# The first spans of an attention and gated feed-forward kernel: instructions put out in the order of a table

## The chip, the cores and the metric

One Trainium2 core runs the whole program. The metric is device time in microseconds (us) of one execution. The trace is one profiled execution on the chip; the times are those of three other executions.

## The reference

```python
# q, k, v: 8 batches x 8 heads x 576 positions x 64, float32
q_s = softmax(q, axis=-1)             # over the 64 columns of a head
k_s = softmax(k, axis=2)              # over the 576 positions
kv = einsum('bhsd,bhse->bhde', k_s, v)
x = einsum('bhsd,bhde->bhse', q_s, kv).transpose(0, 2, 1, 3).reshape(4608, 512)
gate = 1 / (1 + exp(-(x @ w_gate)))   # 512 x 1536
val = x @ w_val                       # 512 x 1536
out = (gate * val) @ w_out            # 1536 x 512
```

The denominators of both softmaxes have 1e-9 added.

## The kernel before

The 4608 tokens are taken in nine spans of 512. A span w needs its 512 rows of x, the two products with w_gate and w_val (called `g1`), the sigmoid and the multiplication, and the product with w_out (`g2`). The 1536 inner columns are taken as 12 tiles j of 128, or six pairs p of tiles.

Span 0 goes tile by tile: `g1_0(j)` on TensorE, `g_sig_0` (L813, ScalarE) and `g_mul_0` (L817, VectorE) make h, and `g2_0(j)` (L855) adds its product with w_out. From tile 5 on the operands are split into a high and a low part, the high part copied on ScalarE, the low part subtracted on VectorE (`h_hi_0`, `h_lo_0`, `wo_hi` L255, `wo_lo` L259, `split_hi` L380, `split_lo` L385). Spans 1 to 8 go pair by pair by a scheme with seven products of sums of blocks (`g1`, L889, then L922 to L951 to put the results together, `g2`, L988). The sums of weight blocks (`w_sums`, L315) and their splits are made once, beside span 0, stored in DRAM, and read back by `s_load` (L399, L401), the first time for two of the pairs unsplit into x_32, and split on arrival (`sums_split`, L342 and L343).

Beside span 0 there is other work. The weights arrive as 64-bit words and are narrowed in four steps that go back and forth between two engines: `w_top` (ScalarE L173), `w_low` (VectorE L178), `w_sign` (ScalarE L187), `w_join` (VectorE L197), and the same as `wo_top`, `wo_low`, `wo_sign`, `wo_join` for w_out. And the attention of span 1 is made: the maxima of k (L428), gathered through a row in DRAM (`k_max_send` L450, `k_max_read` L456), `k_sub` (L482), `k_exp` (L487), `k_sum` (L437), `k_mm`; the maxima, exponentials and sums of q (`qn_max` L594, `qn_sub` L601, `qn_exp` L605, `qn_sum` L611 to L617). For span 2 the maxima of q go to DRAM with `qn_send` (L586) and come back with `q_spread` (L626).

Nothing plans the order: each engine executes its instructions in the order in which the program calls them, and waits at one whose operand is not ready, with all that stands behind it. SP issues the loads, the stores of the result (`acc_out`, L841), `qn_send` and `q_spread`; POOL issues the stores and loads of the split weights. Each of these two queues is in order too, and the transfer that one issues waits for the eighth before it on the same queue. ScalarE needs another function table between an exponential and a sigmoid (ACT_TABLE_LOAD). The calls of span 0 stand in a loop over j whose body calls the steps of different tiles and of the attention in a fixed sequence.

Of the kernel before, what the change touches and what calls it, by code (L numbers as in the profile page):

```python
# [47 lines left out]
C_PAIRS = {T1: T2, B21: T3, B22: T4}  # L48


@with_exitstack
def attn_moe(ctx: ExitStack, tc: tile.TileContext, q0_in, qf, qn, qT, k0T_in, v0_in, k, kT, v, w_in, wo, out):
    nc = tc.nc
# [51 lines left out]
    ctx.enter_context(tc.manual_schedule())  # L105

# [41 lines left out]

    def load_w(j):
        w_raw[j] = t = raw_tile(j)  # L150
        src = w_in[j].bitcast(I32)
        if j:
            nc.sync.dma_start(out=t, in_=src)
        else:
            for n in range(2):
                nc.sync.dma_start(out=half_of(t, n), in_=half_of(src, n))

    def load_wo(j):
# [60 lines left out]

    def w_top(j, n=None):  # L220
        narrow_top(raw_of(j, n), w_of(j, n))

    def w_low(j, n=None):
        w_bits[j, n] = narrow_low(raw_of(j, n))

    def w_sign(j):
        narrow_sign(w_bits[j, None], w_of(j, None))

    def w_join(j, n=None):
        narrow_join(w_bits.pop((j, n)), w_of(j, n))  # L230
# [5 lines left out]

    def wo_top(j):
        if j % 2 == 0:
            wo_t[j // 2] = wtpool.tile([P, 2, DM], F32, name="wo_t")
        narrow_top(in_two(wo_raw[j]), wo_f32(j))  # L240

    def wo_low(j):
        wo_bits[j] = narrow_low(in_two(wo_raw.pop(j)))

    def wo_sign(j):
        narrow_sign(wo_bits[j], wo_f32(j))

    def wo_join(j):
        narrow_join(wo_bits.pop(j), wo_f32(j))

    wo_out = {}

    def wo_hi(j):
        wo_out[j] = t = whpool.tile([P, 2, DM], F32R, name="wo_hl")
        nc.scalar.copy(out=halves(t[:, 0]), in_=apart(wo_t[j // 2][:, j % 2]))  # L255

    def wo_lo(j):
        t = wo_out[j]
        nc.vector.tensor_tensor(  # L259
            out=halves(t[:, 1]), in0=apart(wo_t[j // 2][:, j % 2]),  # L260
            in1=halves(t[:, 0].bitcast(F32)), op=ALU.subtract,
        )

    def wo_store(j):
        t = wo_out[j]
        nc.gpsimd.dma_start(out=wo_dram[j], in_=t.rearrange("p h e -> p (h e)").bitcast(F32))
# [3 lines left out]

    def wo_keep(j):
        nc.gpsimd.dma_start(out=wo_dram[j][:, DM:], in_=wo_t[j // 2][:, j % 2])
# [4 lines left out]

    def wo_load(w, p):
# [13 lines left out]

    def wo_split(w, p):
# [14 lines left out]

    def w_sums(p):
# [20 lines left out]

    def sums_keep(p):
# [4 lines left out]
    s_stage = {}  # L336

    def sums_split(p, parts=range(4)):
# [5 lines left out]

    def sums_store(p, parts=range(4)):
        n = 4 * 2 * P
# [26 lines left out]

    def split_hi(p, parts=(*SUMS, FIRST, LAST)):
# [6 lines left out]

    def split_lo(p, parts=(*SUMS, FIRST, LAST)):
# [11 lines left out]

    def s_load(p, i, first):
# [19 lines left out]

    def kT_load(b, hp, t=None):
# [17 lines left out]

    def k_sum(b, hp):
# [6 lines left out]

    def k_max_turn(b):
        k_turned[b] = ps = ps_at.tile([P, T], F32, name="at")[:NP, 0:P]
        nc.tensor.transpose(ps, kneg[b], ident)

    def k_max_send(b):
# [5 lines left out]

    def k_max_read(b):
# [4 lines left out]

    def k_load(b, t, kt=None):  # L460
# [5 lines left out]

    def v_load(b, t, vt=None):
# [10 lines left out]

    def k_sub(b, t, eng=nc.vector):
# [3 lines left out]

    def k_exp(b, t):
# [5 lines left out]

    def k_tr_0(hp):
# [10 lines left out]

    def k_get_0(hp):
# [7 lines left out]

    def k_mm_0(ps):
# [10 lines left out]

    def k_mm(b, t):
# [12 lines left out]

    def k_done_0(ps):
# [6 lines left out]

    def k_done(b):
# [8 lines left out]

    def kv_split(b, kv):
# [20 lines left out]

    def qn_load(w, c):
# [3 lines left out]

    def qn_send(w, what):
# [6 lines left out]

    def qn_max(w, c):
# [5 lines left out]

    def qn_sub(w, c, eng=nc.vector):
# [23 lines left out]

    def q_spread(w, what, hp):
# [19 lines left out]

    def qf_tr(w, hp, ps):
# [32 lines left out]

    def x_mm(w, hp):
# [14 lines left out]

    def x_ev(w, hp):
# [6 lines left out]

    def qT_copy(hp):
# [38 lines left out]

    def c_subs():
# [11 lines left out]

    def c_split_hi(i):
# [9 lines left out]

    def c_split_lo(i):
# [20 lines left out]

    def g1_0(j):
# [33 lines left out]

    def h_lo_0(j):
# [5 lines left out]

    def acc_out(w):  # L830
# [12 lines left out]

    def g2_0(j):
# [33 lines left out]

    def g1(w, p, s_next=None):
# [74 lines left out]

    def h_split(w, p):
# [12 lines left out]

    def g2(w, at):
# [219 lines left out]

    kT_sb_0 = [k0T[:, hp] for hp in range(NP)]  # L1190
# [43 lines left out]

    def q_sub_0(i):
# [305 lines left out]
```

## Time and profile before

| | |
|---|---|
| median of three executions | 905.75 us (904.39 to 906.54) |
| the profiled execution | 904.38 us |
| its span | 902.5 us |
| TensorE busy | 880.3 us, 98% |
| VectorE, ScalarE, GpSimd busy | 616.6 us, 500.9 us, 184.0 us |
| granted TensorE clock | 1.0 in all windows |

The span is the part of an execution in which the profiler sees instructions; 1.88 us of the profiled execution lie around it. TensorE is busy nearly always, so the rows below list the places where it is not. A row of a timeline has the start of a run of equal instructions, its length, the engine, line, tiles and count, and in brackets the idle time ahead of it and what ended that. Engines are PE (TensorE), DVE (VectorE), ACT (ScalarE), POOL (GpSimd) and SP.

### The profile page before, as it was taken

The numbers are of one execution on the slowest core, as the hardware profiler recorded it, in microseconds if no ns is written. First come the engines' busy times: TensorE is split into PE (matmuls) and PEld (weight loads), VectorE is DVE, ScalarE is ACT, GpSimd is POOL, SyncE is SP. The second block draws the span as 40 slices with busy tenths as digits, with TensorE's granted clock in tenths as the row PEclk, the third lists the DMA queues.
The fourth block names the chain that finished last, engine by engine and source line by source line (L and its number), as shares of the span: only waits on it lengthen the run. The fifth ranks groups of instructions, "written<-read, shape, count | busy, mean of one in ns | idle before, by whom it ended". The sixth has DMA issues, their size and how long they took to land.

```text
span 902.5 us, 16614 instructions
## 1 busy us (share of the span) xinstructions
PE 880.3 (98%) x6533; PEld 799.0 (89%) x6533; DVE 616.6 (68%) x966; ACT 500.9 (56%) x842; POOL 184.0 (20%) x342
## 2 busy tenths in 40 slices
PE   8998888999999999999999999999999999999998
PEld 6444776999999999999999999999999999999997
DVE  8879879878967577666767677666856674664242
ACT  5895677567656456644664466455735443553222
POOL 0102102333221312212221222112122122212220
PEclk9999999999999999999999999999999999999999
DMA  9997545998999979996999799978997799868772
GB/s 334 391 349 249 192 187 189 330 309 264 328 359 286 328 244 352 350 297 213 336 325 325 221 333 341 334 227 284 345 303 240 230 273 325 245 191 261 223 213 70
DMA packets 88966, 252.62 MB, mean 280 GB/s; under 512 B 12892, under 2 KB 13176, under 8 KB 87480
## 3 DMA queue, kind: packets, MB, share of 16 engines
q0 software_dynamic: 45200, 163.08, 57.1%
q1 hardware_dynamic: 43688, 88.47, 31.6%
q8 instruction: 52, 0.85, 0.4%
q14 instruction: 26, 0.21, 0.1%
HBM read 217.97 MB, written 33.54 MB: 279 GB/s over the span
## 4 chain that ended last, share of the span: by engine, by line
PE 71%; DVE 11%; DMA 7%; ACT 6%; issue 4%; POOL 1%; SPq 0%; DVEq 0%; POOLq 0%; ACTq 0%
PE gv L889 43%; PE acc L988 25%; DMA s<-s_sb 3%; DMA s_sb<-s 2%; PE gv L688 1%; PE at L532 1%; DMA x<-s 1%; DVE s L315 1%; DVE k_neg L428 1%; DMA kmax_b<-kmax_row 1%; DVE a_w L385 1%; DMA lent<-q_in 1%; ACT ring L487 1%; ACT w_raw L187 1%; DVE f_w L197 1%
## 5 line engine op out<-in xcount | busy, mean ns | idle before, releaser
L889 PE MATMUL gv<-c_hl,s_sb 128*128 128x256 f32 x2304 | 275.4, 276 | 2.0 <-DMA s_sb<-s 1.0
L889 PEld LDWEIGHTS gv<-c_hl,s_sb 128*128 128x128 f32 x2304 | 265.9, 192 | 3.4 <-issue 1.6
L889 PE MATMUL gv<-c_hl,a_w 128*128 128x256 f32 x1728 | 217.2, 275 | 1.6 <-DVE c_hl L768 1.3
L889 PEld LDWEIGHTS gv<-c_hl,a_w 128*128 128x128 f32 x1728 | 204.8, 192 | 2.7 <-DVE c_hl L768 1.6
L401 POOL DMA_DIRECT2D s_sb<-s x164 | 89.4, 545 | 274.2 <-PE gv L889 256.6
L988 PE MATMUL acc<-wo_hl,h 128*128 128x512 f32 x589 | 135.5, 380 | 0.0
L988 PEld LDWEIGHTS acc<-wo_t,h 128*128 128x128 f32 x613 | 115.5, 189 | 16.3
L988 PE MATMUL acc<-wo_t,h 128*128 128x512 f32 (+1 forms) x613 | 129.7, 362 | 0.0
L935 DVE TENSOR_TENSOR sg<-gv,sg 128x512 f32<-128x512 f32 x48 | 33.1, 690 | 132.5 <-PE gv L889 132.5
L988 PEld LDWEIGHTS acc<-wo_hl,h 128*128 128x128 f32 x589 | 107.7, 189 | 13.6
L937 ACT COPY sg<-gv 128x512 f32<-128x512 f32 x48 | 28.1, 586 | 95.6 <-PE gv L889 95.6
L922 ACT COPY sg<-gv 128x512 f32<-128x512 f32 x48 | 28.2, 587 | 91.3 <-PE gv L889 91.3
L940 DVE TENSOR_TENSOR sg<-sg 128x512 f32<-128x512 f32 x48 | 33.2, 692 | 52.0 <-ACT sg L937 52.0
L961 DVE TENSOR_TENSOR h<-sg,h 128x1024 fp32r<-128x1024 f32 x48 | 58.9, 1226 | 1.7
L949 DVE TENSOR_TENSOR sg<-sg 128x512 f32<-128x512 f32 x48 | 33.2, 692 | 36.6 <-ACT sg L943 36.6
L943 ACT ACTIVATE sg<-sg 128x512 f32<-128x512 f32 x48 | 30.2, 630 | 44.8 <-DVE sg L942 44.8
L289 POOL DMA_DIRECT2D wo_hl<-wo x44 | 23.8, 541 | 151.6 <-PE acc L988 151.6
L931 ACT COPY sg<-gv 128x512 f32<-128x512 f32 x48 | 28.2, 587 | 35.6 <-PE gv L889 35.6
L928 ACT COPY sg<-gv 128x512 f32<-128x512 f32 x48 | 28.1, 585 | 29.4 <-PE gv L889 29.4
L289 POOL DMA_DIRECT2D wo_t<-wo x45 | 24.8, 550 | 93.1 <-PE acc L988 91.9
L805 PE MATMUL gv<-x,f_w 128*128 128x512 f32 x96 | 42.0, 592 | 0.0
L805 PEld LDWEIGHTS gv<-x,f_w 128*128 128x128 f32 x96 | 18.2, 190 | 23.0 <-issue 21.5
(182 smaller groups left out, 1188.2 us busy)
## 6 DMA issues: line engine op xcount, KB each, us to landing
s_sb<-s POOLq DMA_DIRECT2D x164, 512.0 KB, 6.7
wo_t<-wo POOLq DMA_DIRECT2D x45, 512.0 KB, 6.7
wo_hl<-wo POOLq DMA_DIRECT2D x44, 512.0 KB, 5.5
s<-s_sb POOLq DMA_DIRECT2D x24, 512.0 KB, 7.6
out<-x SPq DMA_DIRECT2D x35, 256.0 KB, 6.8
ring<-k_in SPq DMA_DIRECT2D x28, 256.0 KB, 8.5
ring<-qn_in SPq DMA_DIRECT2D x28, 256.0 KB, 5.5
q_b<-q_m_row SPq DMA_DIRECT2D x56, 128.0 KB, 8.7
```

Of the source, the lines that this page charges most:

```text
L289: nc.gpsimd.dma_start(out=t.rearrange("p h e -> p (h e)"), in_=wo_dram[j].bitcast(F32R))
L401: nc.gpsimd.dma_start(out=s_of(i).rearrange("p h n e -> p (h n e)"), in_=s_dram[p][:, i * n:(i + 1) * n].bitcast(F32R),)
L805: nc.tensor.matmul(ps[n], lhsT=a, rhs=x, start=(kt == 0 and i == 0), stop=(kt == NK - 1 and i == len(pairs) - 1),)
L889: nc.tensor.matmul(ps[:, n], lhsT=lh(kt), rhs=woven(c_hl[i][:, x, kt]), start=(first and n == 0 and kt == 0 and lh is wh and x == 0), stop ...
L922: nc.scalar.copy(out=sg[:, 0], in_=y)
L931: nc.scalar.copy(out=sg[:, 1], in_=y)
L935: nc.vector.tensor_tensor(out=sg[:, 0], in0=rr, in1=sg[:, 0], op=ALU.add)
L940: nc.vector.tensor_tensor(out=sg[:, 3], in0=sg[:, 3], in1=sg[:, 2], op=ALU.add)
L943: nc.scalar.activation(sg[:, 0:2, 0], sg[:, 0:2, 0], AF.Sigmoid)
L949: tt(out=sg[:, 0:2, 0], in0=sg[:, 0:2, 0], in1=sg[:, 0:2, 1], op=ALU.mult)
L961: nc.vector.tensor_tensor(out=lo, in0=sg[:, :, 0], in1=hi.bitcast(F32), op=ALU.subtract)
L988: nc.tensor.matmul(acc[w][m][:, es], lhsT=h[lh][:, i, sl], rhs=woven(o[i][:, rh])[:, ts], start=(at == 0 and i == 0 and lh == 0 and rh == ...
```

## The change

A class records the calls of the program from the first load on, up to pair 2 of span 1, as instructions with the name of the step that calls them, its numbers and a count (`wo_low.5`, `k_exp.1.0`, `g1_0.3@4` for the first four matmuls of a step). At pair 2 it puts them out in the order of one table. What is computed does not change, and TensorE's own order does not either. The order on VectorE changes up to about its 240th instruction, on ScalarE up to the 209th, on the SP queue up to the 85th, on POOL up to the 67th. ScalarE has 46 table loads in all where it had 44: among its first 92 instructions there are eight where there were four, and later two fewer.

```diff
+class Steps:
+    def keep(self, engine, call):
+        name = self.names[-1]
+        last = self.kept[-1] if self.kept else None
+        if engine == "tensor" and last and last[:2] == (engine, name):
+            last[3].append(call)
+            return
+        n = self.count[name] = self.count.get(name, -1) + 1
+        self.kept.append((engine, name, f"{name}:{n}" if n else name, [call]))
+
+    def put(self, order):
+        kept, self.kept = {t: calls for _, _, t, calls in self.kept}, None
+        for t in order.split() or list(kept):
+            name, _, n = t.partition("@")
+            calls = kept[name]
+            for _ in range(int(n or len(calls))):
+                calls.pop(0)()
...
+ORDER = """
+top top:1 top:2 top:3 top:4 top:5 v_load.0.4 load_w.0 load_w.0:1 load_wo.0 top:10 load_w.1 load_wo.1 top:11
...
+"""
...
     ctx.enter_context(tc.manual_schedule())
+    nc = Steps(nc)
...
+    @named
     def load_w(j):
...
     nc.gpsimd.memset(ones, 1.0)
+    nc.kept = []
...
         for at in range(NS):
+            if (w, at) == (1, 2):
+                nc.put(ORDER)
             p = step(w, at)
```

Every instruction that went through the table has line 89 after the change. The first place is ScalarE around the sigmoid of tile 3 (h_0_565 before, h_0_235 after; ring are the rows of k, kt its transposed form, lent another part of that, wo_t and wo_raw w_out, w_raw and f_w the gate and value weights). Before:

```order
L487 ACTIVATE ring_374<-ring_374 128x512
L487 ACTIVATE ring_376<-ring_376 128x512
L487 ACTIVATE ring_378<-ring_378 128x512
L487 ACTIVATE ring_380<-ring_380 128x512
L487 ACTIVATE ring_382<-ring_382 64x512
L437 ACTIVATE kt_0_117,k_sum_528<-kt_0_117,k_neg_527 128x576
L437 ACTIVATE kt_1_118,k_sum_528<-kt_1_118,k_neg_527 128x576
L813 ACT_TABLE_LOAD
L813 ACTIVATE h_0_565<-gv_535 128x512
L173 ACTIVATE wo_t_567<-wo_raw_458 128x512
```

After:

```order
L89 ACTIVATE ring_167<-ring_167 128x512
L89 ACT_TABLE_LOAD
L89 ACTIVATE h_0_228<-gv_224 128x512
L89 CAST w_raw_191<-f_w_227 128x2x512
L89 CAST kv_sb_114<-f_last_120 64x4x64
L89 ACTIVATE h_0_235<-gv_232 128x512
L89 ACTIVATE wo_t_236<-wo_raw_229 128x512
L89 ACTIVATE wo_t_236<-wo_raw_218 128x512
L89 CAST w_raw_203<-f_w_227 128x2x512
L89 ACT_TABLE_LOAD
L89 ACTIVATE lent_158,k_sum_205<-lent_158,k_neg_204 128x576 x2
L89 CAST wo_raw_202<-wo_t_217 128x2x256
```

The sigmoid of tile 3 moved ahead of the exponentials of k and of two of the row sums of k, directly behind that of tile 2, and a table load more stands between it and those.

The second place is VectorE around the multiplication of tile 3 (h_0_565 before, h_0_235 after), with the sums of q (q_r) and the split of x (x_hl). Before:

```order
L197 SCALAR_TENSOR_TENSOR wo_t_453<-wo_t_453,wo_raw_404 128x512
L178 TENSOR_SCALAR w_raw_406<-w_raw_406 128x2x512
L178 TENSOR_SCALAR wo_raw_458<-wo_raw_458 128x2x256
L726 TENSOR_TENSOR x_hl_153<-x_0_149,x_hl_152 128x1024
L561 TENSOR_TENSOR kv_sb_114<-f_last_120,kv_sb_114 64x4x64 x2
L611 TENSOR_REDUCE q_r_587<-ring_182 128x8
L611 TENSOR_REDUCE q_r_587<-ring_184 128x8
L611 TENSOR_REDUCE q_r_587<-ring_186 128x8
L611 TENSOR_REDUCE q_r_587<-ring_188 128x8
L616 TENSOR_SCALAR q_r_587<-q_r_587 128x32
L617 RECIPROCAL q_r_587<-q_r_587 128x32
L817 TENSOR_TENSOR h_0_565<-gv_536,h_0_565 128x512
```

After:

```order
L89 TENSOR_REDUCE k_neg_230<-kt_0_117 128x1
L89 SCALAR_TENSOR_TENSOR f_w_227<-f_w_227,w_raw_203 128x1024
L89 TENSOR_TENSOR s_32_213<-f_w_181,s_32_211 128x512
L89 TENSOR_TENSOR h_0_235<-gv_233,h_0_235 128x512
L89 SCALAR_TENSOR_TENSOR wo_t_236<-wo_t_236,wo_raw_229 128x512
L89 RECIPROCAL q_r_239<-q_r_239 128x32
L89 TENSOR_TENSOR ring_166<-ring_166,q_r_239 128x512
L89 TENSOR_SCALAR k_sum_205<-k_sum_205 128x4
L89 SCALAR_TENSOR_TENSOR wo_t_236<-wo_t_236,wo_raw_218 128x512
L89 TENSOR_TENSOR s_32_244<-s_32_243,f_w_200 128x512
L89 TENSOR_REDUCE k_neg_230<-kt_1_118 128x1
L89 SCALAR_TENSOR_TENSOR wo_t_217<-wo_t_217,wo_raw_202 128x512
```

The multiplication no longer stands behind four sums of q; wo_t_217, the w_out tile of tile 3, is joined eight rows behind it, and the other steps moved out from between.

The third place is the SP queue at the end of span 0, where the results of span 0 (out) are stored, the maxima of q go out (q_m_row) and come back (q_b). Before:

```order
L477 DMA f_last<-v_in 128x512 x2
L477 DMA f_last<-v_in 64x512
L477 DMA v_116<-v_in 128x512
L841 DMA out<-x_112 128x512 x4
L586 DMA q_m_row<-q_m 128x32
L626 DMA q_b<-q_m_row 64x512 x8
```

After:

```order
L89 DMA q_m_row<-q_m 128x32
L89 DMA out<-x_112 128x512
L89 DMA ring<-k_in 128x512
L89 DMA out<-x_112 128x512
L89 DMA v_116<-v_in 128x512
L89 DMA q_b<-q_m_row 64x512
L89 DMA out<-x_112 128x512 x2
L89 DMA kt_118<-kT_in 128x576
```

The store of the maxima moved ahead of the four stores of the result, and one reading of them back (q_b) now stands ahead of the last two of these stores.

## Rows read from the trace of the kernel before

**Rows 1.** Part 1 of the page: busy time, share, instructions.

```profile
PE 880.3 (98%) x6533; PEld 799.0 (89%) x6533; DVE 616.6 (68%) x966; ACT 500.9 (56%) x842; POOL 184.0 (20%) x342
```

**Rows 2.** Windows; PE, PEld, DVE, ACT, POOL busy (count), granted clock, DMA share, GB/s.

```profile
23.50:68.40 44.90, 44.88 (x106) 19.54 (x104) 35.26 (x52) 39.09 (x58) 5.94 (x10) 1.00 0.99 370
68.40:181.30 112.90, 99.73 (x574) 79.83 (x575) 98.35 (x154) 73.70 (x112) 23.25 (x41) 1.00 0.64 229
181.30:902.50 721.20, 716.01 (x5684) 683.84 (x5682) 463.89 (x734) 373.98 (x647) 153.97 (x285) 1.00 0.92 281
```

**Rows 3.** Timeline of TensorE: start, length, what, idle time ahead and releaser.

```profile
61.35 7.03 PE L805 MATMUL gv<-x,f_w 128*128 128x512 f32 x16
71.85 3.70 PE L855 MATMUL acc<-wo_t,h 128*128 128x512 f32 x8 [3.47 <-DVE h L817]
...
110.29 5.94 PE L805 MATMUL gv<-x_hl,a_w 128*128 128x512 f32 x24 [1.38 <-ACT v L813]
...
148.07 2.86 PE L855 MATMUL acc<-wo_hl,h_parts 128*128 128x512 f32 x12 [0.29 <-ACT h_parts L821]
...
152.38 1.49 PE L889 MATMUL gv<-c_hl,a_w 128*128 128x256 f32 x11 [1.35 <-DVE c_hl L768]
...
155.76 1.60 PE L889 MATMUL gv<-c_hl,s_sb 128*128 128x256 f32 x12 [0.55 <-ACT sg L922]
...
162.84 2.75 PE L855 MATMUL acc<-wo_hl,h_parts 128*128 128x512 f32 x12
...
171.85 3.11 PE L889 MATMUL gv<-c_hl,s_sb 128*128 128x256 f32 x24 [0.59 <-DMA s_sb<-s]
...
182.66 2.84 PE L889 MATMUL gv<-c_hl,s_sb 128*128 128x256 f32 x24
```

**Rows 4.** Waits of TensorE over the span: total, times, longest.

```profile
PE acc L855 <- DVE wo_hl L259: 3.1, 3, 1.1
PE gv L805 <- DVE a L385: 2.2, 2, 1.7
```

**Rows 5.** Chain of waits from 40 to 75 us: start, length, what.

```profile
50.66 6.69 DMA kmax_b<-kmax_row
...
58.10 3.03 ACT ring L487 x5
...
62.66 1.28 ACT L813
63.96 0.60 ACT h L813
...
68.18 2.48 DVE q_r L611 x4
...
71.16 0.63 DVE h L817
```

**Rows 6.** Lines by form, VectorE, 23.5 to 68.4 us: busy time, mean ns.

```profile
L197 DVE SCALAR_TENSOR_TENSOR f_w<-f_w,w_raw 128x1024 int32<-128x1024 int32 x2 | 2.4, 1220 | 1.1 <-ACT w_raw L187 1.1
...
L315 DVE TENSOR_TENSOR s<-f_w 128x512 f32<-128x512 f32 x2 | 1.4, 684 | 0.0
```

**Rows 7.** Timeline of VectorE from 160 to 170 us.

```profile
167.55 2.45 DVE L594 TENSOR_REDUCE q_m<-ring 128x8 f32<-128x512 f32 x4
```

**Rows 8.** Waits of the SP queue, 20 to 200 us: total, times, longest.

```profile
SPq L626 <- DMA q_m_row<-q_m: 8.1, 1, 8.1
```

**Rows 9.** Timeline of the SP queue from 160 to 185 us.

```profile
165.59 3.11 SPq L841 DMA_DIRECT2D out<-x  x4
```

**Rows 10.** DMA issues from 148 to 153 us: size, us to landing.

```profile
kmax_b<-kmax_row POOLq DMA_DIRECT2D x1, 256.0 KB, 4.0
kmax_row<-kmax_b POOLq DMA_DIRECT2D x1, 2.0 KB, 2.8
```

**Rows 11.** DMA issues from 150 to 190 us: size, us to landing.

```profile
x<-s POOLq DMA_DIRECT2D x8, 256.0 KB, 6.6
out<-x SPq DMA_DIRECT2D x4, 256.0 KB, 9.0
```

More of the change, by code (lines that the diff above doesn't have):

```diff
@@ L48, with __init__ @@
 C_PAIRS = {T1: T2, B21: T3, B22: T4}
+class Steps:
+    def __init__(self, nc):
+        self.kept, self.names, self.count = None, ["top"], {}
+        for e in ("tensor", "vector", "scalar", "gpsimd", "sync"):
+            setattr(self, e, Engine(self, e, getattr(nc, e)))
+    def keep(self, engine, call):
[13 more added lines that the diff above has]
+                calls.pop(0)()
+        assert not any(kept.values()), [t for t, calls in kept.items() if calls]
@@ new lines, with __init__, __getattr__, call @@
+class Engine:
+    def __init__(self, steps, name, engine):
+        self.steps, self.name, self.engine = steps, name, engine
+    def __getattr__(self, op):
+        do = getattr(self.engine, op)
+        def call(*args, **kw):
+            if self.steps.kept is None:
+                do(*args, **kw)
+            else:
+                self.steps.keep(self.name, lambda: do(*args, **kw))
+        return call
+ORDER = """
+top top:1 top:2 top:3 top:4 top:5 v_load.0.4 load_w.0 load_w.0:1 load_wo.0 top:10 load_w.1 load_wo.1 top:11
@@ new lines @@
+split_hi.4.1.2.3.4:2 wo_sign.10 g1_0.9@12 g_sig_0.9 top:23 w_sign.11 qT_split.1.3:1 g1_0.9 g_mul_0.9
+w_join.11 split_lo.5.0 split_hi.4.1.2.3.4:1 g2_0.8 split_hi.4.1.2.3.4:3 split_lo.4.1.2.3.4:2
+split_hi.4.1.2.3.4 x_mm.1.3 h_hi_0.9 split_lo.4.1.2.3.4 split_hi.5.6.5 split_lo.4.1.2.3.4:4 wo_hi.9
+wo_join.10 split_lo.4.1.2.3.4:5 wo_lo.9 split_lo.4.1.2.3.4:1 wo_hi.10 split_lo.4.1.2.3.4:3 h_lo_0.9 x_ev.1.3
+wo_store.9 wo_low.11 c_split_hi.0 w_sums.5 split_hi.5.6.5:1 c_split_lo.0 g1_0.10@12 g_sig_0.10 w_sums.5:2
@@ new lines @@
+g1_0.10 split_lo.5.6.5:1 split_lo.5.6.5 c_subs:2 split_hi.5.1 w_sums.5:1 wo_sign.11 g2_0.9 g_mul_0.10
+split_lo.4.1.2.3.4:6 h_hi_0.10 wo_lo.10 split_hi.5.2.3.4:1 split_hi.5.2.3.4 w_sums.5:3 wo_load.1.4:1 top:22
+split_lo.4.1.2.3.4:7 c_subs:1 h_lo_0.10 c_subs:3 g1_0.11 split_lo.5.2 k_max_turn.2 c_split_hi.1 split_lo.5.1
+split_lo.5.2:1 c_split_hi.4 wo_store.10 g_sig_0.11 split_lo.5.1:1 c_split_hi.2 g_mul_0.11 g2_0.10
+c_split_lo.1 c_split_lo.4 g1.1.5.4 g1.1.5.4:1 c_split_lo.2 c_split_hi.3 wo_join.11 g1.1.5.4:2
@@ L105, in attn_moe, with named, step @@
     ctx.enter_context(tc.manual_schedule())
+    nc = Steps(nc)
+    def named(f):
+        def step(*args, **kw):
+            numbers = [a for x in args for a in (x if isinstance(x, tuple) else (x,)) if isinstance(a, (int, str))]
+            nc.names.append(".".join(map(str, (f.__name__, *numbers))))
+            f(*args, **kw)
+            nc.names.pop()
+        return step
     def r(ap):
@@ L240, in wo_top @@
         narrow_top(in_two(wo_raw[j]), wo_f32(j))
+    @named
     def wo_low(j):
         wo_bits[j] = narrow_low(in_two(wo_raw.pop(j)))
+    @named
     def wo_sign(j):
         narrow_sign(wo_bits[j], wo_f32(j))
+    @named
     def wo_join(j):
```

127 lines of the change are left out of this document (added).

## Prediction

> **What bounds the kernel now.** I read part 1 of the page first: TensorE is busy for 880.3 of 902.5 us [rows 1], so whatever the order does, at most 22 us are to be had. The windows say where. From 181.3 us on, beyond the table's reach on TensorE, TensorE is busy for 716.0 of 721.2 us, and from 23.5 to 68.4 us for 44.88 of 44.90; in between it idles for 112.90 − 99.73 = 13.2 us [rows 2]. The granted clock is 1.00 in all three. The timeline of TensorE then shows this idle time as eleven waits: 3.47, 1.09, 1.38, 1.03, 0.57, 1.00, 1.67, 0.29, 1.35, 0.55 and 0.59, together 12.99 us [rows 3, 4]. I call them a to k; b, d and f are the three for wo_hl, and e and g the two for `a`, that rows 4 add up. Ten of them end on an instruction of VectorE or ScalarE, the last on a DMA. VectorE is busy for 35.26 of 44.90 and then for 98.35 of 112.90 us, ScalarE for 39.09 and 73.70 [rows 2]: neither is full, so the waits come from what stands ahead of the operand that is wanted, and an order can remove them.
>
> The longest, a, is followed on the chain of waits [rows 5]. The maxima of k land at 50.66 + 6.69 = 57.35. Five subtractions begin there, and ScalarE then does five exponentials (3.03), two row sums, the table load (1.28), and only then the sigmoid of tile 3, at 63.96. VectorE, having got its next piece from ScalarE, still does splits and four sums of q (2.48) ahead of the multiplication of tile 3, which starts at 71.16. TensorE had finished the matmuls before its need at 61.35 + 7.03 = 68.38 [rows 3].
>
> **The change part by part.** TensorE keeps its order and its matmuls; all that can change is how long it waits. I went through the new order with the durations of the trace of before, each instruction behind its predecessor and its operands, against the times at which TensorE would need them without any wait.
>
> *Wait a.* In the new order the sigmoid of tile 3 follows that of tile 2, and the multiplication follows a join and a sum; of the five exponentials none stands ahead of the sigmoid, and the sums of q are done earlier. The last feed of `g2_0(3)` is then not the multiplication but the join of its w_out tile, eight rows behind. Up to it VectorE has 60 instructions from 23.5 us on: 42 of 0.68 us, 8 wide ones of 1.21, one reduction of 2.5, nine small ones of together 3.3, 44.2 us end to end; the two frequent sizes are those of [rows 6]. They overlap: four sums take 2.48, or 0.62 each [rows 5], which takes off 60 × 0.06 = 3.6. So 40.6 us of work stand in the 44.9 us up to 68.4. VectorE did 35.26 there and waited for 9.64 [rows 2]; it may now wait for 4.3. ScalarE has 45 instructions up to the piece that this join needs, 39 us end to end and 35 with a like overlap of 0.09, in the same 44.9. I get the join 1.9 us ahead of time: a goes, −3.47. If VectorE waits as much as before, 9.64 − 4.3 = 5.3 comes back, more than a; that end stays in the range.
>
> *Waits b to j.* Here the wanted low part, product or sum is moved forward among independent work. In the walk the operands come ahead of need by 1.1 (h_lo of tile 5), 0.9 and 2.5 (the blocks `a`), 1.6 (c_hl, the one behind the wait of 1.35), about 3 (wo_hl) and 1.2 to 2 (the rest). They sum to 8.93. The margins are of the size of one or two VectorE instructions (0.68 to 1.22 [rows 6]), and one handover that comes a row late costs that much. I let a fifth come back: +1.8. Bounds: 0, and all 8.9.
>
> *Wait k and the SP queue.* TensorE's product with the sums of the next pair starts at 182.66 in before [rows 3]; its second sum is wanted half of the 2.84 later, so at 184.1 − 13.0 = 171.1 without waits. It comes through a line of transfers that the change makes longer: the store of the maxima of q, then a reading of them back, then two stores of the result behind this in the SP queue, and only then can x_32 be loaded anew. In before that reading waits 8.1 us for the store to land [rows 8], but with all four stores of the result ahead; nothing of it is behind. After, `g2_0(11)` ends at 162.84 + 2.75 − 12.4 = 153.2 [rows 3], two copies and two reductions of 2.45 / 4 = 0.61 each follow [rows 7], and the store goes at 155.7. From there: landing, three issues on SP at 3.11 / 4 = 0.78, together 2.3 [rows 9], landing of the result, landing of the load, 1.3 for the split, two instructions of the shorter size of [rows 6]. With short landings, 2.8 for the store and 4.0 for each 256 KB [rows 10], this is 155.7 + 2.8 + 2.3 + 4.0 + 4.0 + 1.3 = 170.1, 1.0 early. With crowded ones, 8.1 [rows 8], 9.0 and 6.6 [rows 11], it is 183.0, 11.9 late. The store now goes ahead of the four results, so its landing is nearer to 2.8; the other two are in the same traffic as before, and I take 6.6 for each: 175.3, 4.2 late, less the 1.8 by which TensorE is late by then, and less another 0.9, an estimate, because DMA is busy for only 0.64 of this window [rows 2] and 6.6 may be too long: +1.5. Wait k itself (0.59) goes.
>
> By the Trainium skill, "DMA: Bandwidth & Descriptors", section "Anatomy of one DMA — SWDGE (gpsimd) path", a DMA takes about 2.0 us and its bytes at 436 GB/s, 2.6 us for 256 KB. The 6.6 and 9.0 of [rows 11] don't agree, since other transfers run beside them. By the rule the line would end at 155.7 + 2.0 + 2.3 + 2.6 + 2.6 + 1.3 = 166.5, 4.6 us early, the term of 1.5 would be nothing, and the sum 1.5 lower.
>
> *Table loads.* Four more of them stand in ScalarE's first 92 instructions, two fewer later. One takes 1.28 us, and the sigmoid behind it starts 0.02 us after its end [rows 5], so 4 × 1.28 = 5.1 us of ScalarE, which the 5.8 us that it idles from 23.5 to 68.4 and the 39.2 us after that hide [rows 2]; those that fall ahead of the join are counted in its 35 us. Cost 0. The cover is gone where a sigmoid is late by more than its margin, 2.4 us at tile 2.
>
> The Trainium skill speaks against this: "ScalarE: Activation LUTs", "What ACT_TABLE_LOAD costs" and "Table sets: the hidden batching unit", counts 2.66 us for each switch, load and drain, and asks to batch by set. The row shows no drain of 1.38 us. By the page the four cost 10.6 us of ScalarE, and the margin of tile 2 shrinks by 1.4 for the one switch ahead of it; it is not used up.
>
> *Start and tail.* Up to 23.5 us the order is almost the same, and behind 181.3 us it is unchanged: 0.
>
> Sum: −12.99 + 1.8 + 1.5 = −9.7. The profiled execution took 904.38, so 894.7; the median of the shown runs lies 1.37 above it, so 905.75 − 9.7 = 896.0.
>
> **The rivals.** *A, half the waits return.* Margins of 1 to 2 us are small on two in-order engines that hand each piece back and forth. Half of 12.99 is 6.5: 899.3. For it: ten of the eleven waits are of this kind. Against: VectorE idles 24.2 us from 23.5 to 181.3 [rows 2], and 11 of them would remain without any wait on TensorE.
>
> *B, the SP queue replaces them.* If the landings are as in [rows 8, 11], TensorE waits up to 11.9 at the second sum; the 1.8 is inside this, so −12.99 + 11.9 = −1.1 and 904.7 at the far end, 898.7 with half of it. For it: these landings are from this very stretch. Against: the store no longer goes last.
>
> *C, slower: VectorE starves.* The place is 23.5 to 95 us, where each narrowing goes ScalarE, VectorE, ScalarE, VectorE, now with exponentials and table loads between, and where a load that lands late stops both engines in turn; some weights are now requested behind other loads, while DMA is at 0.99 of its time [rows 2]. It decides from the point where VectorE idles more than the 24.2 us of before up to the end of the table; each us above is one on TensorE. With 28 us it is 905.75 + 3.8 = 909.5. Against: VectorE would have to wait for 17 us more than the new order's work leaves.
>
> *D, given back later.* The main part needs DMA at 0.92 of its time [rows 2]; if it is this that sets its end, an earlier start only waits for loads: 905.75. Against: at 281 GB/s TensorE idles there for only 5.2 us in 721.
>
> **How the numbers follow.** Forecast 0.55, A 0.18, B 0.13, C 0.09, D 0.05. What a measurement of this kernel can tell from no change is about 0.2%, 1.8 us: faster means below 903.9. The forecast but for 0.01, A, and most of B (0.11) are faster, 0.83; D, 0.01 of the forecast and 0.02 of B are the same, 0.08; C is slower, 0.09. The lowest sum has neither term come back and half a us more of the start: 905.75 − 13.0 − 0.7 = 892.0. Upwards, A and the half of B lie under 903.5; what is beyond, with C, D and the far end of B, is 0.2.
>
> **What would show it.** Right: the window from 68.4 to 171 us has TensorE idle for 2 to 4 us, `g2_0(3)` follows the matmuls of tile 4 without a gap, VectorE waits for 10 to 15 us up to the end of the table, and the main part keeps its 721 us. For the term of the SP queue: the wait ahead of the second sum of the next pair, with a load of x_32 as its releaser. Wrong: new waits on TensorE of over 1 us behind products or low parts (A), over 4 us at that sum (B), more idle time than 24 us on VectorE (C), or a longer main part (D).

## The result, and the profile after

| | before | after |
|---|---|---|
| median of five executions | 905.75 us (904.39 to 907.26) | 894.57 us (890.31 to 896.62) |
| ratio, 95% interval | | 0.9871 (0.9841 to 0.9900) |
| the profiled execution, its span | 904.38, 902.5 us | 894.13, 892.3 us |

The forecast was 896.0. In the windows of the changed kernel the middle one ends at 164.65, where TensorE does what it did at 181.30 in [rows 2]; the columns are those of [rows 2].

```profile
23.50:68.40 44.90, 44.90 (x107) 19.77 (x106) 42.38 (x65) 42.79 (x58) 7.37 (x14) 1.00 0.96 342
68.40:164.65 96.25, 95.40 (x574) 80.23 (x573) 89.57 (x140) 73.80 (x114) 19.99 (x37) 1.00 0.77 276
164.65:892.30 727.65, 717.66 (x5684) 685.35 (x5682) 465.56 (x735) 373.46 (x647) 153.51 (x285) 1.00 0.93 279
```

The counts of matmuls in the last two rows, 574 and 5684, are those of before. The middle stretch takes 96.25 us instead of 112.90, 16.65 less, and TensorE idles there for 0.85 instead of 13.2. The main part takes 727.65 instead of 721.20: 6.45 are given back in it. VectorE is now busy for 42.38 of the first 44.90 us. The timeline of TensorE, for [rows 3]:

```profile
68.16 3.60 PE L89 MATMUL acc<-wo_t,h 128*128 128x512 f32 x8
...
146.11 0.94 PE L89 MATMUL gv<-c_hl,a_w 128*128 128x256 f32 x6 [0.47 <-ACT sg L89]
...
151.35 2.92 PE L89 MATMUL gv<-c_hl,s_sb 128*128 128x256 f32 x24 [0.37 <-DMA s_sb<-s]
...
172.32 2.72 PE L87 MATMUL gv<-c_hl,s_sb 128*128 128x256 f32 x22 [1.92 <-DVE s_sb L87]
...
179.92 1.76 PE L87 MATMUL at<-f_last,ring 128*64 128x64 f32 x48 [2.46 <-DMA f_last<-v_in]
181.61 4.54 PE L87 MATMUL acc<-wo_hl,h 128*128 128x512 f32 x12
```

The product of tile 3 with w_out starts at 68.16 without a gap, 3.69 earlier than in [rows 3]. Of a to k none is left; in the table's reach there are waits of 0.47 and 0.37, both at places where before had none. Then two come that before did not have: 1.92 ahead of the third sum of the next pair, whose releaser is VectorE, and 2.46 ahead of the last rows of v of batch 2. The 12 matmuls at 181.61 take 4.54 us; 13 of the same shape, at 185.99, take 2.76. The granted clock says why (windows, the clock is the third figure from the right):

```profile
177.50:179.90 2.40, 0.00 (x0) 0.01 (x1) 0.48 (x1) 2.39 (x5) 0.00 (x0) 1.00 1.17 302
...
181.50:185.50 4.00, 4.00 (x17) 3.15 (x13) 3.97 (x6) 0.59 (x2) 0.00 (x0) 0.57 1.08 328
185.50:189.00 3.50, 3.50 (x21) 3.13 (x20) 3.11 (x7) 0.00 (x0) 0.00 (x0) 1.00 0.31 100
```

It was 0.50, that is 1.2 GHz, for most of the stretch from 181.5 to 185.5, behind a wait in which TensorE did nothing for 2.4 us. From the wait ahead of the third sum to the end of the slow stretch the lead over before shrinks from 16.67 (173.57 before, 156.90 after) to 10.5.

Behind the waits a to j the lead is 16.6 us (157.37 before, 140.79 after), though these add up to 12.4 on TensorE. Where the rest comes from is seen on its weight loads, which wait for the same operands. Before, from 68 to 165 us (what waited, for whom, in total, times, longest):

```profile
PEld acc L855 <- DVE wo_hl L259: 4.3, 3, 1.5
PEld acc L855 <- DVE h L817: 4.3, 1, 4.3
...
PEld gv L805 <- DVE a L385: 3.0, 2, 2.1
PEld gv L889 <- DVE c_hl L768: 1.6, 1, 1.6
PEld gv L805 <- ACT v L813: 1.6, 1, 1.6
PEld gv L805 <- DVE v L817: 1.0, 3, 0.4
```

After:

```profile
PEld gv L89 <- ACT sg L89: 0.7, 1, 0.7
PEld gv L89 <- PE gv L89: 0.5, 1, 0.5
```

The rows of before with an engine as releaser come to 18.6 us, six shorter ones among them; those of after to 1.2. On the timeline of TensorE a wait counts from the modelled end of the matmul before. The three waits for wo_hl are 3.1 there [rows 4] and 4.3 here; the lead grew by 3.9 at them. At wait a it is 3.47, 4.3 and 3.6. So the matmuls show too little, and the weight loads somewhat too much.

### The profile page after: what moved, and what is told of

Same layout as the page of the kernel before. It is cut to its first block, busy times and chain, and to the rows that moved or that the text cites. A ratio compares the mean times of both kernels' runs of the same rounds, so it can differ in the third digit from the quotient of the medians.

```text
span 892.3 us, 16606 instructions
## 1 busy us (share of the span) xinstructions
PE 877.2 (98%) x6533; PEld 800.7 (90%) x6533; DVE 616.7 (69%) x966; ACT 504.3 (57%) x844; POOL 181.7 (20%) x342
## 4 chain that ended last, share of the span: by engine, by line
PE 88%; DMA 4%; DVE 2%; issue 2%; ACT 1%; POOL 1%; SPq 0%; POOLq 0%; DVEq 0%; ACTq 0%
PE gv L87 46%; PE acc L87 26%; PE gv L89 10%; PE acc L89 4%; DMA s<-s_sb 2%; PE at L87 2%; DMA ring<-k_in 1%; DMA s_sb<-s 1%; PE at L89 1%; DMA lent<-q_in 1%; DVE lent L89 0%; DVE q_r L89 0%; DVE q_m L89 0%; DVE ring L87 0%; ACT ring L87 0%
## 5 line engine op out<-in xcount | busy, mean ns | idle before, releaser
L87 PE MATMUL gv<-c_hl,s_sb 128*128 128x256 f32 x2208 | 263.3, 276 | 2.7 <-DVE s_sb L87 1.9
L87 PEld LDWEIGHTS gv<-c_hl,s_sb 128*128 128x128 f32 x2208 | 254.6, 192 | 3.5 <-DVE s_sb L87 2.6
L87 PE MATMUL gv<-c_hl,a_w 128*128 128x256 f32 x1656 | 207.8, 275 | 0.3 <-ACT x L87 0.3
L87 PEld LDWEIGHTS gv<-c_hl,a_w 128*128 128x128 f32 x1656 | 196.1, 192 | 0.6 <-ACT x L87 0.6
L87 DVE TENSOR_TENSOR sg<-gv,sg 128x512 f32<-128x512 f32 x138 | 82.8, 600 | 133.2 <-PE gv L87 131.3
L87 DVE TENSOR_TENSOR sg<-sg 128x512 f32<-128x512 f32 x138 | 79.1, 601 | 86.9 <-ACT sg L87 86.8
L87 ACT ACTIVATE sg<-sg 128x512 f32<-128x512 f32 x92 | 43.0, 515 | 43.4 <-DVE sg L87 43.3
L87 ACT ACTIVATE ring<-ring 128x512 f32<-128x512 f32 (+1 forms) x86 | 46.9, 619 | 0.1
L87 DVE TENSOR_TENSOR ring<-ring,q_b 128x512 f32<-128x512 f32 x56 | 35.9, 686 | 6.5 <-DMA q_b<-q_r_row 3.0
L87 DVE CAST h<-sg 128x1024 fp32r<-128x1024 f32 x46 | 31.8, 692 | 1.2
```

Of the source, the lines that this page charges most:

```text
L87: do(*args, **kw)
```

## The experiments

Twelve kernels ran. Spans are those of the profiled execution, medians those of the timed ones, each beside the kernel before on the same chip. The profiled execution is one of these: the slowest for e2_tail and e3_kt_last, the fastest for e4_k_ahead, e6_by_need, e8_switch and e11_same. So where spans differ by few us, the ratios decide.

| kernel | span | median | ratio to before, 95% interval |
|---|---|---|---|
| before | 902.5 | 905.75 | |
| after | 892.3 | 894.57 | 0.9871 (0.9841 to 0.9900) |
| e1_head | 901.1 | 902.91 | 0.9975 (0.9961 to 0.9988) |
| e2_tail | 900.3 | 900.80 | 0.9930 (0.9906 to 0.9953) |
| e10_k_late | 903.1 | 904.59 | 0.9992 (0.9984 to 1.0001) |
| e7_pad | 900.9 | 904.01 | 0.9984 (0.9973 to 0.9995) |
| e8_switch | 894.1 | 897.02 | 0.9901 (0.9887 to 0.9916) |
| e4_k_ahead | 894.6 | 897.92 | 0.9910 (0.9895 to 0.9925) |
| e3_kt_last | 892.9 | 892.36 | 0.9852 (0.9834 to 0.9871) |
| e5_v_ahead | 888.4 | 891.05 | 0.9836 (0.9822 to 0.9851) |
| e6_by_need | 887.7 | 891.68 | 0.9838 (0.9823 to 0.9852) |
| e9_mix | 889.3 | 891.37 | 0.9838 (0.9821 to 0.9856) |
| e11_same | 893.2 | 896.30 | 0.9901 (0.9888 to 0.9914) |
| e12_split | 886.6 | 888.45 | 0.9821 (0.9801 to 0.9842) |

**The table's head alone (e1_head), its tail alone (e2_tail).** In e1_head the table's first 252 entries are followed by the other calls in the old order; e2_tail puts the same 252 entries out in the old order and then the rest of the table.

```diff
-        for t in order.split() or list(kept):
+        head = order.split()
+        head = head[:head.index("g2_0.3") + 1]
+        for t in head + list(kept):
```

```diff
+        for t in [f"{t}@{early[t]}" for t in kept if early.get(t)] + steps[cut:]:
```

e1_head: 

> The first 252 entries of the table, up to the product of tile 3 with w_out, are put out in the table's order, and all that follows in the order of before. Theory: the gain comes wait by wait, so this kernel loses wait a (3.47 of idle time and 0.1 of a slower start after it) and keeps most of b to k; some of these shrink, as work was pulled ahead of the cut. Span 902.5 - 3.6 to 902.5 - 7, so 895.5 to 899. Rival: the gain is one of the whole (the early part alone only shifts the idle time to the next wait): span above 901. The wait ahead of the third sum of the next pair and the one on the last v load, both new after the change, are not there, since the queue's order is the old one.

e2_tail: 

> The converse: the calls of those first 252 entries are put out in the order of before, the rest in the table's. Theory: wait a stays near 3.5, waits b to k are gone as in the changed kernel, and the two new waits at 172 and 180 us (there 1.9 and 2.5) shrink by what TensorE comes later, to about 0, because the loads that they wait for do not depend on wait a. So the span comes out near the changed kernel's 892.3, at 892 to 894, though a wait of 3.5 has come back. Rival: gains add up, and the span is 892.3 + 3.7 = 896.

The head won its 3.6 (68.23 for 71.85) and kept 1.4 of it. The waits of the old order stayed, at their old sizes:

```profile
PE acc L91 <- DVE wo_hl L91: 3.1, 3, 1.1
PE gv L91 <- DVE a L91: 2.2, 2, 1.7
PE gv L91 <- ACT v L91: 1.5, 2, 1.4
```

The expected 895.5 to 899 was wrong, and the rival's sign, a span above 901, was there: the work that the head pulls forward shortens nothing behind it, and 2.2 of the 3.6 went later on, 1.0 of them by 182 us. In e2_tail wait a was gone too, against what I expected, because four of the five exponentials of k and two of the five subtractions don't belong to the calls ahead of the cut and so came later; the matmuls of k and v then waited for them:

```profile
85.19 1.12 PE L95 MATMUL at<-v,ring 128*64 128x64 f32 x16 [2.56 <-ACT ring L95]
...
187.15 3.02 PE L93 MATMUL at<-f_last,ring 128*64 128x64 f32 x48 [6.51 <-DMA f_last<-v_in]
```

The second row is the wait for the last rows of v, 6.5 and not 0: these were issued at 176.8, since the SP queue's end comes later by what the rest comes later, and more. The clock was 0.50 from 183.9 to 194.1, and of a lead over before of 12.8 us at 161 us 1.7 was left.

In these executions the head is worth 1.4 us of span and the tail 2.2, together 3.6, and the whole table 10.2. But at TensorE's place of 173.57 in before their leads are 2.6, 12.8 and 16.7 (wait a is gone in all three, so this is no clean split): the difference arises behind it, where the last rows of v are late. And the executions of e2_tail go from 895.39, at a granted clock of 0.999, to the profiled 902.15, at 0.992. By the timed ratios the head is worth 0.25%, the tail 0.70% and the whole 1.29%, or 0.99% when it was timed again (e11_same). That the parts are worth less than the whole isn't shown.

**One move in the old loop (e10_k_late).** 

> The kernel before, with one move in the loop: the five subtractions and five exponentials of k of span 1 come in iteration 4, behind the multiplication of tile 3, instead of in iteration 3 ahead of it. Theory (wait a is these ten standing ahead of the multiplication): a falls from 3.47 to under 0.7, and no new wait of 1 us follows before 105 us, unless the matmuls of k and v at 82 us now wait for the exponentials (they waited 2.6 for them where only the table's tail was used). Of what is won, most is given back behind 181 us, as with the table's head (3.6 won, 1.4 left): span 900 to 902.5. Rival: a is of VectorE being full, and the wait moves one tile on: the shift at 90 us is under 1.

```diff
-        if j == 3:
+        if j == 4:
             for t in range(5):
                 k_sub(1, t)
             for t in range(5):
                 k_exp(1, t)
+        if j == 3:
             load_next(1, 3)
```

Wait a went (68.30 for 71.85), so the ten instructions ahead of the multiplication were its cause. The 3.55 were gone by 98 us:

```profile
73.36 7.13 PE L805 MATMUL gv<-x,f_w 128*128 128x512 f32 x16 [1.47 <-DVE f_w L197]
...
93.98 1.99 PE L855 MATMUL acc<-wo_hl,h_parts 128*128 128x512 f32 x8 [0.60 <-DVE wo_hl L259]
```

The next wait came at the next products, for the join of their weights. Ahead of that join stand, on ScalarE and VectorE:

```profile
67.79 3.03 ACT L487 ACTIVATE ring<-ring 128x512 f32<-128x512 f32 x5 [4.24 <-DVE ring L482]
```

```profile
72.08 1.23 DVE L197 SCALAR_TENSOR_TENSOR f_w<-f_w,w_raw 128x1024 int32<-128x1024 int32 x1 [1.92 <-ACT w_raw L187]
```

ScalarE idled for 4.24 until the moved subtractions were made, did the five exponentials, and only then the sign step (L187) that the join waits for; VectorE idled for 1.92. So the ten instructions now stood ahead of the next narrowing, and this wait isn't one of a full VectorE, as the rival had it. Both forecasts were missed: theory had no new wait of 1 us and a span of 900 to 902.5, the rival a shift of under 1 at 90 us, where it was 1.8. The median shows no difference.

**A fuller VectorE (e7_pad).** 

> The changed kernel, in which each of the four sums of q of span 1 on VectorE is made four times instead of once: 12 more reductions of 0.62, 7.4 us, all ahead of the join of the w_out tile 3. VectorE has 44.9 - 42.4 = 2.5 us of idle time from 23.5 to 68.4 us. Theory (VectorE is nearly full in this stretch, so the margin is 2 to 2.5 us and what is above comes out as waits on TensorE): waits of 4 to 6 us between 45 and 85 us, span 896 to 899. Rival (VectorE works ahead and the margin is larger): less than 3 us of waits there, span under 895.

```diff
-                self.steps.keep(self.name, lambda: do(*args, **kw))
+                more = op == "tensor_reduce" and self.steps.names[-1].startswith("qn_sum.1.")
+                self.steps.keep(self.name, lambda: [do(*args, **kw) for _ in range(1 + 3 * more)])
```

```profile
59.18 3.70 PE L90 MATMUL acc<-wo_t,h 128*128 128x512 f32 x8 [1.01 <-DVE h L90]
65.84 8.80 PE L90 MATMUL gv<-x,f_w 128*128 128x512 f32 x16 [2.96 <-DVE q_r L90]
```

Waits of 1.01 and 2.96, together 4.0, the lower end of what was expected; but 16 matmuls then took 8.80 us instead of 7.03, at a granted clock of 0.62 from 65.8 to 70.3. The shift at 64 us is 6.3 of the 7.4 that were added, and the whole gain of the change but 0.16% is gone. The span of 900.9 is over the expected 896 to 899: 6.3 us against the change stay up to 172 us, and 2.3 more came behind a wait of 3.12 ahead of the last matmuls of k and v, with the clock at 0.50 from 186.2 to 193.0. The margin is small, as the theory had it.

**Two more table loads (e8_switch).** 

> The changed kernel with an exponential of one column between the sigmoids of tiles 2 and 3, and so two more table loads in the fullest stretch of ScalarE. Theory by the rows (a switch is 1.28 us and no drain): ScalarE takes 2 x 1.28 + 0.2 = 2.8 us more there, the sigmoid of tile 3 comes 2.8 later, and TensorE waits for nothing: span 892 to 893. By the page of the Trainium skill on activation tables it would be 2 x 2.66 + 0.2 = 5.5 us, which ScalarE's 2.1 us of idle time in this stretch don't hide: a wait of 1 us or more on TensorE before 85 us.

```diff
         nc.scalar.activation(h_0[j], gate[j][0], AF.Sigmoid)
+        if j == 2:
+            nc.scalar.activation(pad_c[:, 1:2], ident[:, 1:2], AF.Exp)
```

The timeline of ScalarE in that kernel:

```profile
51.37 1.28 ACT L89 ACT_TABLE_LOAD   x1
52.66 0.20 ACT L89 ACTIVATE pad_c<-ident 128x1 f32<-128x1 f32 x1
...
54.54 1.28 ACT L89 ACT_TABLE_LOAD   x1
55.84 0.60 ACT L89 ACTIVATE h<-gv 128x512 f32<-128x512 f32 x1
```

A load takes 1.28, and the instruction behind it starts 0.01 to 0.02 later. The 1.38 us of draining that the Trainium skill counts ("ScalarE: Activation LUTs", "What ACT_TABLE_LOAD costs") don't show at either switch. The sigmoid of tile 3 came at 55.84 instead of 54.63, since ScalarE had idled for 1.65 ahead of it, and TensorE waited for nothing new before 165 us. The span is 894.1 all the same, over the expected 892 to 893: the wait for the last rows of v was 3.8 in this execution, behind an earlier arrival (the wait ahead of the third sum was 0.7). That this comes of the table loads isn't shown; the timed ratio, 0.9901, is that of the changed kernel in e11_same.

**The two new waits (e4_k_ahead, e3_kt_last, e5_v_ahead).** VectorE around the wait of 1.92 in the changed kernel:

```profile
166.68 0.68 DVE L89 TENSOR_TENSOR ring<-ring,q_m 128x512 f32<-128x512 f32 x1
170.38 1.28 DVE L89 TENSOR_TENSOR ring<-ring,kmax_b 64x512 f32<-64x512 f32 x2 [3.01 <-DMA ring<-k_in]
171.59 1.28 DVE L87 TENSOR_TENSOR s_sb<-x,s_sb 128x512 fp32r<-128x512 f32 x2
```

and the SP queue:

```profile
157.12 1.05 SPq L89 DMA_DIRECT2D out<-x  x2
162.31 0.34 SPq L89 DMA_DIRECT2D kt<-kT_in  x1
162.74 1.03 SPq L89 DMA_DIRECT2D ring<-k_in  x1
...
169.72 0.34 SPq L89 DMA_DIRECT2D kt<-kT_in  x1
...
171.03 0.41 SPq L89 DMA_DIRECT2D f_last<-v_in  x1
```

What the two loads of kt waited for on that queue:

```profile
SPq L89 <- ACT kt L89: 4.1, 1, 4.1
SPq L89 <- DMA kt<-kT_in: 2.2, 1, 2.2
```

The split of the third sum (171.59) stands behind a subtraction that waits for the last k rows; these stand on SP behind a load of k of batch 3, which waits until 162.3 for ScalarE. The last v rows go at 171.03 behind a second load of k and land at 179.8. That second load waits for no engine: it goes at 169.72, when the first, the eighth transfer before it, has landed (169.66).

```text
e4_k_ahead: ... k_load.2.4 kT_load.3.1 ...        (k_load.2.4 was behind)
e3_kt_last: ... q_spread.2.m.3:1 kT_load.3.1 kT_load.3.0
e5_v_ahead: ... v_load.2.2 kT_load.3.0 ...        (v_load.2.2 was behind)
```

e4_k_ahead: 

> The changed kernel, with only the load of the last k rows of batch 2 (k_load.2.4) moved ahead of kT_load.3.1; the last v load stays where it is. Theory: the subtraction no longer waits, the wait ahead of the third sum (1.9) goes, but TensorE then comes to the last rows of v 1.9 earlier, while these land as before: that wait grows from 2.5 to about 4.4, and the span stays at 892 to 893. Rival (each wait is a cost of its own): span 890.4.

```profile
179.87 3.02 PE L87 MATMUL at<-f_last,ring 128*64 128x64 f32 x48 [4.01 <-DMA f_last<-v_in]
```

The wait ahead of the third sum went, and the one for v grew to 4.0 from 2.5, as the theory had it. The clock then stayed at 0.50 until 188, longer than in the changed kernel, and the span rose to 894.6, over the expected 892 to 893: in this execution an earlier arrival at a fixed landing cost 2 us more. The timed ratio, 0.9910, can't be told apart from the changed kernel's 0.9901 in e11_same.

e3_kt_last: 

> The changed kernel, with the two loads of k of batch 3 (kT_load.3.1, kT_load.3.0) moved from the middle of the SP queue to the end of the table. Theory: in the changed kernel the first of them held up the queue from 158.2 to 162.3 and the second to 169.7, and the last rows of k and v of batch 2 behind them came late: VectorE waited 3.0 at the subtraction of the last k rows, with the split of the third sum behind it (1.9 on TensorE), and TensorE waited 2.5 for the last rows of v, after which it ran at half its clock for some 3 us (about 2 us). Both waits and the slow stretch go: 1.9 + 2.5 + 2.0 = 6.4 less, span 886 to 888. Rival: the waits are the transfers' own (DMA is over 1.0 busy there), and moving two loads of 288 KB behind only moves what is late: span 890 to 893. Second rival: the time comes back in the main part, which then starts earlier on the same loads: span 890 to 892, with the two waits gone.

Both waits went, and in this execution the first rival held. With nothing that stops the SP queue, 1.7 MB were issued on it from 158 to 163.5; the second load of x_32, issued at 161.4 in place of 161.0, landed 5 us later, and ScalarE stood at its split, with the copy that frees TensorE's accumulator behind it:

```profile
164.76 0.62 ACT L89 CAST s_sb<-x 128x512 fp32r<-128x512 f32 x1 [1.10 <-DMA x<-s]
170.53 0.62 ACT L89 CAST s_sb<-x 128x512 fp32r<-128x512 f32 x1 [5.15 <-DMA x<-s]
171.05 0.58 ACT L87 COPY sg<-gv 128x512 f32<-128x512 f32 x1
```

```profile
171.68 2.93 PE L87 MATMUL gv<-c_hl,s_sb 128*128 128x256 f32 x12 [3.58 <-ACT sg L87]
174.40 2.77 PE L87 MATMUL gv<-c_hl,a_w 128*128 128x256 f32 x12
```

A wait of 3.58, and again matmuls at half the clock. This execution is the slowest of four, 894.65 at a granted clock of 0.996; the two fastest took 891.0 at 1.000. So that the move wins nothing is shown for the one execution; by the timed ratio, 0.9852, it is no slower than the change.

e5_v_ahead: 

> The changed kernel, with only the last load of v rows of batch 2 (v_load.2.2) moved ahead of kT_load.3.0 on the SP queue, one place. In the changed kernel it was issued at 171.0 and landed at 179.9; ahead of kT_load.3.0 it can go at about 167.5 and lands at 176 to 177.5, where TensorE wants it at 177.5. Theory: the wait of 2.5 goes, and with it the stretch at 1.2 GHz from 181.5 to 185.5 (2.1 us); the wait ahead of the third sum (1.9) stays. Span 892.3 - 4.6 = 887.7. Rival (transfers only change places, as when both k loads went to the end): another wait of 2 us or more comes up between 160 and 180 us, and the span is 890 to 893.

```profile
178.01 1.76 PE L87 MATMUL at<-f_last,ring 128*64 128x64 f32 x48 [0.40 <-DMA f_last<-v_in]
```

The row for v is 0.4, the clock 1.00 throughout, the span 888.4. The load went at 169.46 and not at 167.5, since in this place too it goes when the first load of kt has landed (169.44). One DMA moved one place is worth 3.9 us of span between these two executions, more than its wait of 2.5; by the timed ratios it is 0.9836 against 0.9871, or 0.9901 in e11_same.

**The queue in the order of need (e6_by_need, e9_mix, e12_split).**

```text
e6:  stores, k_load.2.4, 4 v loads, 8 q_b, 2 qT, kT_load.3.1, kT_load.3.0
e9:  stores, k_load.2.4, kT_load.3.1, 4 v loads, 8 q_b, 2 qT, kT_load.3.0
e12: stores, k_load.2.4, 4 q_b, kT_load.3.1, 4 v loads, 4 q_b, 2 qT, kT_load.3.0
```

e6_by_need: 

> The changed kernel, with the SP queue of the table's end in the order in which the data is wanted: the four stores of the result, then the last rows of k and v of batch 2, and behind them all eight q_b, the two qT and the two kT loads of batch 3. With kT alone moved, the loads of x_32 got slower, since 1.7 MB were issued within 6 us of them; here 0.9 MB of that goes behind. Theory (the wait is set by what is issued together with x_32): x_32 lands 2 us earlier than in that kernel, the wait of 3.6 there falls to 1 or less, no clock drop, the rows of v are in time: span 886 to 889. Rival (x_32 waits for the stores of the result, which free it, not for its neighbours): its second load is issued at 160 instead of 161.4 at best and the wait is 2 to 3.5: span 890 to 893.

The span is in the range, but the wait at x_32 was 1.46 and not under 1.

e9_mix: 

> The changed kernel with another order at the table's end on the SP queue: the stores of the result, the last k rows (k_load.2.4), then kT_load.3.1, which waits until 162.3 us for ScalarE and so holds the rest back while x_32 is loaded; behind it the four v loads, the q_b, the qT and the other kT load. Theory (x_32 must come without neighbours, the v rows by 175): x_32 lands at 165.4 as in the changed kernel, the last k rows before 166, the last v rows at 174 to 176; no wait of 1 us or more between 150 and 182 us, no stretch at 1.2 GHz. Span 885.5 to 887, under both kernels where the queue was changed in one way only (888.4 and 887.7). Rival: a wait of 1 to 2 us stays in another place and the span is 887.5 to 889.

All waits from 150 to 182 but 0.2 went, and 6.5 us were won there; then a qT load was late for VectorE, TensorE waited at 202.5, and the clock was 0.50 from 203.4 to 206.8. The span of 889.3 is over both forecasts:

```profile
187.76 0.69 DVE L87 TENSOR_TENSOR ring<-ring,q_b 128x512 f32<-128x512 f32 x1 [1.21 <-DMA ring<-qT_in]
189.67 0.69 DVE L87 TENSOR_TENSOR ring<-ring,q_b 128x512 f32<-128x512 f32 x1 [1.22 <-DMA ring<-qT_in]
```

```profile
202.50 2.19 PE L87 MATMUL gv<-c_hl,s_sb 128*128 128x256 f32 x12 [2.74 <-ACT sg L87]
```

e12_split: 

> As e9_mix, but four of the eight q_b loads stand ahead of kT_load.3.1 instead of behind the v loads. In e9_mix no wait was left from 150 to 182 us (6.5 us ahead of the changed kernel there), but the q_b and qT loads were issued up to 4 us later, VectorE waited for a qT load from 185 to 190 us, and TensorE then waited 2.7 at 202.5 and ran at half its clock behind that. Theory: the queue's total is fixed, so four q_b within the 5 us in which it stands at kT_load.3.1 bring all that follows forward by about 4 us; the wait at 202.5 goes and 5 to 6.5 us stay: span 886 to 887.5. Price looked for: x_32 has four more neighbours of 128 KB, and may land 1 us later, with a wait of up to 1.5 at 168 us: span 888. Rival: with DMA over its time in this stretch each order has its own late transfer, and no order of the queue alone gets under 887.5.

One wait of over 0.5 us is left there, 1.20 at x_32; the clock is 1.00 from 150 to 187. The rival's bound of 887.5 is passed by 0.9 us in this execution and by three of the five; the other two have spans of 888.4. It is the lowest of all medians, 0.9821 of before against 0.9871 for the change, with intervals that just touch, and 0.9901 in e11_same, clear of it; from e5_v_ahead and e6_by_need it can't be told apart.

**The same kernel again (e11_same).** 

> The changed kernel once more, beside e9_mix on the same chip. Its executions spread from 890.3 to 896.6. If the last v rows and the clock behind them make this spread, the wait for these rows differs from 2.5 in this profile, and the shift between its two profiles arises between 160 and 190 us and not elsewhere.

```profile
180.13 1.76 PE L87 MATMUL at<-f_last,ring 128*64 128x64 f32 x48 [2.80 <-DMA f_last<-v_in]
181.82 2.86 PE L87 MATMUL acc<-wo_hl,h 128*128 128x512 f32 x12
...
205.96 1.60 PE L87 MATMUL gv<-c_hl,s_sb 128*128 128x256 f32 x12 [1.44 <-ACT sg L87]
```

The wait for v was 2.8, near 2.5, but the 12 matmuls behind it took 2.86 us and not 4.54: the granted clock stayed at 1.00. The two traces differ by less than 0.25 us up to 182. Then this one is 1.5 ahead at 186, has lost that by 250, most of it in waits at 206 and 223 us (1.44 and 0.83, where the other has 0.63 and 0.32), and is 0.9 behind from 302 us on. So the wait is repeatable, and the fall of the clock behind it is not, in the same program; and what the faster clock won was waited for later. The spread of the medians, 894.57 and 896.30, isn't explained by this wait. Of the executions of the changed kernel the fastest, 890.31, has a granted clock of 1.000 and the others, 894.13 to 896.62, have 0.997 to 0.998; here 894.94 goes with 0.999 and 898.02 with 0.994. What makes the clock fall in one execution and not in another isn't shown.

## Why the prediction was right

The time came out as forecast, and the part on the waits a to k holds in its mechanism. The part on what stands behind them does not, and the sum is right by luck.

- *The waits go.* Right: a to k are gone, and what came instead is 0.84, where 1.8 was forecast. The term itself was mis-sized: I took 12.99, the idle time that the timeline of TensorE shows, 12.4 of it for a to j, and 16.6 were won at these. Part of a wait lies under the modelled end of the matmul before it, and the first matmuls behind a wait start further apart (8 behind wait a take 3.70 us [rows 3], and 3.60 without it): three waits for wo_hl are 3.1 on TensorE, and the lead grew by 3.9 at them.
- *Wait a and VectorE.* Right: the join of the w_out tile ended at 66.2, 1.95 ahead of need (1.9 in the walk), and VectorE idled for 2.5 us up to 68.4, less than the 4.3 allowed. e7_pad shows that not much more was to be had.
- *The SP queue, +1.5.* The size was near, 2.1 with the slower start, but by luck: the place was one sum late, and the mechanism was wrong. The store of the maxima landed after 3.0 us, as the row to which it was nearest said, the store of the result whose landing the trace has after 3.3 instead of a median of 9.0, and x_32 was in time. What was late were the last k rows, behind a load that waits for ScalarE, and VectorE's head of line did the rest. The step that failed is "only then can x_32 be loaded anew" as the line that sets the end; With other orders of the queue this line did come: x_32 was late in e3_kt_last (3.58), e6_by_need (1.46) and e12_split (1.20).
- *Tail, 0.* Wrong: I counted the order behind 181.3 as unchanged and forgot that the table also orders loads whose data the unchanged part wants. Its wait of 2.46 for v and the 1.7 us at half the clock behind it are 4.2 of the 6.45 that the main part gave back. The 1.7 are no fixed price: in e11_same the clock stayed up behind 2.8, and other waits took the time. That the two loads were late is shown by e4_k_ahead and e5_v_ahead, which moved one each and lost the wait for it.
- *Table loads, 0.* Right as far as e8_switch shows: with two loads more TensorE waited for nothing new before 165 us.
- *The sum.* −16.7 at 157 us with the residue in it, then +2.1, +2.4 for v and +1.7 for the clock, and 0.3 of smaller waits: −10.2, against −9.7. Two errors of about 5 us had opposite signs, and that they cancel is luck. Of the signs named ahead, TensorE's idle time from 68.4 to 171 us was 1.45 and not 2 to 4, VectorE's up to 171 us was 12.7, within 10 to 15, and the main part took 727.65 and not 721. Of A there is one wait, the 1.92 behind a low part; C did not happen; of B the place was one sum off and the cause was another; D holds in part, since 6.45 were given back, though for loads at the seam and not by the main part's own need of DMA: from 250 us to the end the lead over before stays at 10.0 to 10.6.

## What to carry to other kernels

A wait is worth more than the idle time of the matmuls, and here less than that of the weight loads: 12.4, 18.6, and 16.6 won. An order written for one stretch also sets when loads for the next one go: follow each load past the place where the new order ends, and ask on its queue which entry ahead of it waits for an engine, or for the landing of an earlier transfer. What is won ahead of a late load is not kept: TensorE only waits longer for it (e2_tail, e4_k_ahead). And one profiled execution can mislead about a kernel: those of e2_tail go from 895.4 to 902.2 us.

## What the runs showed of the hardware

A wait on TensorE of 2.46 to 6.51 us was followed by matmuls at 1.2 GHz in seven profiles: until 185.1 after the 2.46 in the changed kernel, until 188.4 after the 4.01 in e4_k_ahead. After 0.4, 1.20, 1.46 and 1.92 the clock stayed at 2.4 GHz, and also after the 3.47 of wait a in the kernel before and after the 2.80 in e11_same, the same program as the changed kernel. So the length of the wait alone doesn't decide; what does was not tried. Where it falls, 1.3 to 4.0 us come on top of the wait (1.3 behind the 2.56 in e2_tail, 4.0 in e4_k_ahead). A load on the SP queue that stands and waits for an engine spaced out the transfers behind it, and x_32 landed earlier for it, at 165.4 and not at 170.5 (e3_kt_last); in that execution taking this stop away cost as much as it won. A transfer also waited for the landing of the eighth before it on its queue: the second load of kt went at 169.72, behind a landing at 169.66, the v load of e5_v_ahead at 169.46, behind one at 169.44. And a table load took ScalarE 1.28 us, with the next instruction 0.01 to 0.02 behind it (e8_switch).
